# Merged DMA transposes for two head pairs in a pooled attention with a multiplicative feed-forward behind it

## The chip, the cores and the metric

The kernel runs on one core of a Trainium2 chip. The metric is the device time of one execution in microseconds (us), lower is better; the time before is the median of five executions.

## The reference

Attention with pooled queries, and then a feed-forward network without an activation function. Inputs are float32; the output is 4608 x 512 float32.

```python
B, H, S, D = 8, 8, 1152, 64
q_pool = q.reshape(B, H, S // 2, 2, D).mean(axis=3)            # 576 queries per head
scores = (1 / sqrt(D)) * q_pool @ k.transpose(0, 1, 3, 2)      # 576 x 1152 per head
attn = softmax(scores)
x = (attn @ v).transpose(0, 2, 1, 3).reshape(B * 576, 512)     # tokens x (head, D)
out = ((x @ w1) * (x @ w2)) @ w3 @ w_out                       # w1, w2: 512x1024, w3: 1024x1024, w_out: 1024x512
```

## The kernel before, in words

**Pairs.** Two heads at a time make a pair; there are 32 pairs (`NP`), four for each of the 8 batch entries. All matrix products are in fp16 with float32 accumulation. A pair's keys come in as 128 partitions x 2 heads x 9 rows x 64 (`kst`), its queries as 64 partitions x 2 x 18 x 64 (`qst`, two pairs share one tile of 128 partitions), its values like its keys (`vst`). GpSimd issues these loads (`load_k`, `load_q`, `load_v`); they convert float32 to fp16 on the way.

**Preparation of a pair.** VectorE copies the keys into `kc`, so that the two heads lie side by side, adds neighbouring queries into `qp` (`pool_q`), and copies the values into one of four standing tiles (`copy_v`). Keys and queries must then be transposed to `kT` and `qT`, with the head dimension on the partitions. For pairs 0 to 7 TensorE does it (`prep_first`, `prep_groups`). From pair 8 (`NPE`) on, `prep_dma` does it for two pairs at a time with DMA transposes, issued from SyncE's queue (SP): nine 128x128 tiles for the keys of the first pair (line 140), nine for the queries of both (line 143), nine for the keys of the second (line 140 again). `settled` (line 146) then lets GpSimd read one element of each of the three results, and only after that GpSimd issues the six loads of the two pairs that come next (`load_two`), so that these loads don't start beside the transposes.

**Scores and exponentials.** The main loop makes three chunks (`BURST`) of 512 columns each time: `scores` (line 248) multiplies keys by queries into a PSUM tile of tag `psc`, of which there are three, and ScalarE writes the exponentials into a ring `er` (line 258). A pair has 10.125 chunks.

**Attention times values.** `attend` (line 272) multiplies `er` by the values: 90 small matmuls a pair (2 heads x 9 key rows x 5 column groups), with a column of constants that gives the sum of the exponentials. The fifth column group overlaps the fourth: its upper 64 rows are the last 64 of the 576 queries. How many of these matmuls each turn of the loop issues stands in a list written out by hand (`PVS`). `normalize` (lines 285 and 289) divides by the sum and writes `xn`.

**Transposing the result.** `turn_x` issues two DMA transposes a pair: four 128x128 tiles (line 303) and a 64x128 piece for the last 64 queries (line 306). They write `xT`, the feed-forward network's input. For an odd pair this follows its `normalize`; even pairs from 8 on are put into `held` and turned at a later turn of the loop (line 552).

**Feed-forward.** Nine units of 512 tokens. A unit multiplies `xT` by w1 (`pa`) and w2 (`pb`, line 371); VectorE copies `pa` to `asb` (line 381) and multiplies it by `pb` into `gT` (line 383); then `gT` is multiplied by `T16`, the product of w3 and w_out that is made early (`pp`, line 389), VectorE scales it into `osb` (line 401), and SP stores it (line 410), two DMAs for every 128 tokens. The groups of up to seven units are put between the scores and the attention matmuls of the main loop, in one PSUM bank of their own ("F") or in one of the three `psc` slots ("X"); the last units run as a tail with ScalarE's help.

**What sets the order.** The program runs in manual order: every engine executes its instructions in the order in which the Python code emits them, and waits for the others by semaphores. So a wait of VectorE or of SP holds all that is behind it on that engine. Transposes and stores go through SP's queue, loads through GpSimd's; all of them share the core's 16 DMA engines.

Of the kernel before, what the change touches and what calls it, by code (L numbers as in the profile page):

```python
# [8 lines left out]
FP16 = mybir.dt.float16  # L9
# [5 lines left out]
SQ = 576  # L15
NJ = 9
# [3 lines left out]
VW = 66  # L20
# [3 lines left out]
def kernel(  # L24
# [11 lines left out]
    nc = tc.nc  # L36
    B, H, S, D = q.shape
# [5 lines left out]
    NP = B * H // 2  # L43
    SCL = 16.0
    NPE = 8
# [3 lines left out]
    const = ctx.enter_context(tc.tile_pool(name="const", bufs=1))  # L49
    stage = ctx.enter_context(tc.tile_pool(name="stage", bufs=4))  # L50
    ab = ctx.enter_context(tc.tile_pool(name="ab", bufs=4))
# [4 lines left out]
    xT = const.tile([128, NC, NT], FP16)  # L56
# [4 lines left out]
    er = const.tile([128, 2, RING], FP16)  # L61
    vts = [const.tile([128, 2, NJ, VW], FP16, name=f"vt{i}") for i in range(4)]

    ident = const.tile([128, 128], FP16)
    seen = const.tile([1, 3], FP16)

    ctx.enter_context(tc.manual_schedule())

# [1 line left out]
        nc.vector.memset(vt[:, :, :, D:VW], 1.0 / SCL)  # L70


    kst, vst, qst, kT, qT, qTs, qps = {}, {}, {}, {}, {}, {}, {}

    def load_q(P):
        b, h0 = P // 4, 2 * (P % 4)
# [36 lines left out]
    def pool_q(P, n=1):  # L113

        pp, o = P // 2, 64 * (P % 2)
        if P % 2 == 0:
            qps[pp] = ab.tile([128, NJ, 2, D], FP16, tag="qp", bufs=2, name="qp")
        r = slice(o, o + 64 * n)
        src = qst[pp][r].rearrange("p u (c two) d -> p u c two d", two=2)
        nc.vector.tensor_tensor(  # L120
            out=qps[pp][r].rearrange("p c u d -> p u c d"),
            in0=src[:, :, :, 0, :], in1=src[:, :, :, 1, :], op=ALU.add)

    def new_kq(P):
        kT[P] = ab.tile([128, NJ, 128], FP16, tag="kT", bufs=4, name="kT")
        if P % 2 == 0:
            qTs[P // 2] = ab.tile([128, NJ, 128], FP16, tag="qT", bufs=2, name="qT")
        o = 64 * (P % 2)
        qT[P] = qTs[P // 2][:, :, o:o + 64]

    def copy_v(P):
# [2 lines left out]
    def prep_dma(P):  # L134

        for p in (P, P + 1):
            new_kq(p)
            kc = ab.tile([128, NJ, 2, D], FP16, tag="kc", bufs=2, name="kc")
            nc.vector.tensor_copy(out=kc.rearrange("p j u d -> p u j d"), in_=kst.pop(p))
            nc.sync.dma_start_transpose(out=kT[p], in_=kc.rearrange("p j u d -> p (j u d)"))  # L140
            if p == P:
                pool_q(P, 2)
                nc.sync.dma_start_transpose(
                    out=qTs[P // 2], in_=qps[P // 2].rearrange("p c u d -> p (c u d)"))

    def settled(P):
        for n, t in enumerate((kT[P], qTs[P // 2], kT[P + 1])):
            nc.gpsimd.tensor_copy(out=seen[:, n:n + 1], in_=t[0:1, 0, 0:1])  # L148

    kcs = {}  # L150

    def new_kc(P):
        kcs[P] = ab.tile([128, NJ, 2, D], FP16, tag="kc", bufs=2, name="kc")
        return kcs[P]

    def prep_stage(P):
# [79 lines left out]
    def scores(c):  # L236
        t = psum.tile([128, 2, CH], FP32, tag="psc", bufs=3, name="psc")
        psc[c] = t
        g = c * CH
        while g < (c + 1) * CH:  # L240
            J = g // SQ
            P, j = divmod(J, NJ)
            f0 = g - J * SQ
            ln = min(SQ - f0, (c + 1) * CH - g)
            o = g - c * CH
            for u in range(2):
                s = slice(64 * u, 64 * u + 64)
                nc.tensor.matmul(t[:, u, o:o + ln].rearrange("p (c f) -> p c f", f=64), kT[P][s, j, :],  # L248
                                 qT[P][s, f0 // 64:(f0 + ln) // 64], start=True, stop=True)
            g += ln  # L250

    def expo(c):
        r = (c * CH) % RING
        g = (c - RING // CH + 1) * CH
        if g > 0:
            Pg, Jg = divmod((g - 1) // SQ, NJ)
            assert nb >= 90 * Pg + 45 + 5 * Jg + 5
        nc.scalar.activation(out=er[:, :, r:r + CH], in_=psc.pop(c), func=AF.Exp,  # L258
                             bias=0.0, scale=SCALE)

    po, xns = {}, {}

    def attend(n):

        P, m = divmod(n, 90)
        u, m = divmod(m, 45)
        j, i = divmod(m, 5)
        if m == 0:
            po[P, u] = psum.tile([128, 512], FP32, tag="po", bufs=1, name="po")
        f = 128 * i if i < 4 else SQ - 128  # L270
        r = ((P * NJ + j) * SQ) % RING + f
        nc.tensor.matmul(  # L272
            po[P, u][:, VW * i:VW * i + D + 1], er[:, u, r:r + 128],
            vts[P % 4][:, u, j, 0:D + 1],
            start=(m == 0), stop=(m == 44), skip_group_check=True)

# [5 lines left out]
    def normalize(P, u):  # L282
        acc = po.pop((P, u))[:, 0:5 * VW].rearrange("p (i w) -> p i w", w=VW)
        rz = ab.tile([128, 5, 1], FP32, tag="rz", bufs=2, name="rz")
        nc.vector.reciprocal(out=rz, in_=acc[:, :, D:D + 1])  # L285
        if u == 0:
            xns[P] = ab.tile([128, 5, 2, D], FP16, tag="xn", bufs=3, name="xn")
        xn = xns[P]
        nc.vector.tensor_tensor(  # L289
            out=xn[:, :, u, :], in0=acc[:, :, 0:D],  # L290
            in1=rz.to_broadcast([128, 5, D]), op=ALU.mult)
        if u == 0:
            return
        if P >= NPE and P % 2 == 0 and P < NP - 2:
            held.append(P)
        else:
            turn_x(P)

    def turn_x(P):
        xn = xns.pop(P)  # L300
        b, hp = divmod(P, 4)
        n0 = b * SQ
        nc.sync.dma_start_transpose(
            out=xT[:, hp, n0:n0 + 512].rearrange("p (i r) -> p i r", r=128),
            in_=xn[:, 0:4].rearrange("p i u d -> p (i u d)"))
        nc.sync.dma_start_transpose(
            out=xT[:, hp, n0 + 512:n0 + SQ].rearrange("p (i r) -> p i r", r=64),
            in_=xn[64:128, 4].rearrange("p u d -> p (u d)"))


    w3h = []
# [50 lines left out]
    def ffn_groups(t):  # L362
# [71 lines left out]
        out=ident, in_=ident, compare_op=ALU.not_equal, fill=1.0,  # L434
# [7 lines left out]
    load(3)  # L442
    load_w3(2)
    loaded, staged, prepped, copied = 4, 1, 1, 1
    held = []
    rest = prep_first()

    n_units = NT // 512
# [37 lines left out]
    def first_it(P):  # L486
        return P * PAIR // (CH * BURST)

    early = [(3, w3_group(0)), (4, w3_group(1))]
    for c in range(NF):  # L490
        t = (6, 7, 8, 9, 11, 12, 14, 15)[c]
# [14 lines left out]
    for it in range(NIT):  # L506
        at = it * BURST * CH / PAIR
        while early and it >= early[0][0]:
            queue.append(early.pop(0)[1])
        while next_unit < EARLY:  # L510
            last_b = (512 * (next_unit + 1) - 1) // SQ
            if it < 3 or reached[it - 2] < 360 * (last_b + 1):
                break
            gens.append(ffn_groups(next_unit))
            next_unit += 1
        for w in range(BURST):
            scores(BURST * it + w)
            expo(BURST * it + w)
        if it == 0:
            prep_rest(rest)  # L520
            load(4)
            load_w3(3)
            loaded = 5
        lead = 2 if staged < 4 else 3
        if staged < NPE and it >= first_it(staged) - lead:
            prep_stage(staged)
            staged += 1
            if staged <= 4:
                load(loaded)
                loaded += 1  # L530
            if staged <= 3:
                load_ffn(staged - 2)
        while 8 <= loaded < NPE + 2 and at >= loaded - 3.4:
            load(loaded)
            loaded += 1
        urgent = False
        if prepped < NPE:
            if it >= first_it(prepped) - (1 if prepped < 4 else 2):
                queue[0:0] = prep_groups(prepped)
                prepped += 1  # L540
                urgent = True
        elif prepped < NP and at >= prepped - 1.25:
            prep_dma(prepped)
            if loaded < NP:
                settled(prepped)
                load_two(loaded)
                loaded += 2
            prepped += 2
        if copied < NP and at >= copied - (1.2 if copied >= NPE else 0.6):
            copy_v(copied)  # L550
            copied += 1
        while held and at >= held[0] + 2.2:
            turn_x(held.pop(0))
        n = PVS[it]
        left = 45 - nb % 45
        brief = bool(queue) and queue[0][2] == 1
        a = left if left < n else 8 if brief and it > 8 and 8 < n < 40 and 8 < left else 0
        assert nb + n <= NPV and ready(nb + n - 1, BURST * it)
        pv(a)
        if head():  # L560
            group("F")
        if head() and (n < 40 or urgent or it < 17):
            group("X")
        pv(n - a)
        reached.append(nb)
    assert not held
    while nb < NPV:
        if head():
            group("F")
# [40 lines left out]
```

## Time and profile before

| | |
|---|---|
| time, median of 5 executions | 431.87 us (429.6 to 432.33) |
| profiled execution | 432.07 us, span 430.3 us |
| TensorE matmuls (PE) | 406.4 us, 94% of the span |
| ScalarE (ACT) | 326.6 us, 76% |
| VectorE (DVE) | 211.0 us, 49% |
| GpSimd (POOL) | 80.3 us, 19% |
| GpSimd's DMA queue (loads) | 48.3% of the 16 DMA engines' span |
| SP's DMA queue (transposes, stores) | 32.4% |
| granted TensorE clock, mean | 0.996 |

A time "busy" is the union of an engine's instructions. DMA issues count as no engine's work; SP's queue has a row for each, from the issue's start, and the trace tells when its data had landed. In rows of the timeline the bracket at the end says how long the engine had been idle and whose work ended that. Rows of a table by stretches give, after the length, busy us and instructions of PE, PE's weight loads, DVE, ACT and POOL, then the granted clock, the busy share of the DMA engines, and GB/s.

### The profile page before, as it was taken

The numbers are of one execution on the slowest core, as the hardware profiler recorded it, in microseconds if no ns is written. First come the engines' busy times: TensorE is split into PE (matmuls) and PEld (weight loads), VectorE is DVE, ScalarE is ACT, GpSimd is POOL, SyncE is SP. The second block draws the span as 40 slices with busy tenths as digits, with TensorE's granted clock in tenths as the row PEclk, the third lists the DMA queues.
The fourth block names the chain that finished last, engine by engine and source line by source line (L and its number), as shares of the span: only waits on it lengthen the run. The fifth ranks groups of instructions, "written<-read, shape, count | busy, mean of one in ns | idle before, by whom it ended". The sixth has DMA issues, their size and how long they took to land.

```text
span 430.3 us, 12736 instructions
## 1 busy us (share of the span) xinstructions
PE 406.4 (94%) x5432; PEld 269.5 (63%) x5432; DVE 211.0 (49%) x442; ACT 326.6 (76%) x355; POOL 80.3 (19%) x146
## 2 busy tenths in 40 slices
PE   3989999899999999799989999799999999999996
PEld 1667777666685577466765587466756776544443
DVE  1456565556536563456355554555465635623130
ACT  4898899879888888589878898788888899223332
POOL 8333321040401204030403012213004000000000
PEclk9999999999999999899999999999999999999999
DMA  8999999987895959997695969998958862040404
GB/s 126 205 208 200 188 180 172 152 153 123 126 201 114 179 88 165 218 148 126 98 201 104 161 122 185 169 189 119 218 116 122 112 147 40 15 100 12 99 1 98
DMA packets 95625, 59.16 MB, mean 137 GB/s; under 512 B 66256, under 2 KB 85968, under 8 KB 95568
## 3 DMA queue, kind: packets, MB, share of 16 engines
q0 software_dynamic: 26544, 33.56, 48.3%
q1 hardware_dynamic: 68864, 24.66, 32.4%
q8 instruction: 42, 0.69, 0.7%
q10 hardware_dynamic: 160, 0.13, 0.1%
q14 instruction: 15, 0.12, 0.1%
HBM read 67.11 MB, written 9.44 MB: 178 GB/s over the span
## 4 chain that ended last, share of the span: by engine, by line
PE 67%; DMA 26%; DVE 2%; POOL 2%; issue 2%; SPq 0%; ACT 0%; DVEq 0%; POOLq 0%
PE po L272 15%; PE pa L371 14%; PE pb L371 14%; PE psc L248 13%; PE pp L389 11%; DMA qst<-in_q_dram 7%; DMA vst<-in_v_dram 6%; DMA w2sb<-in_moe_w_dram 5%; DMA kst<-in_k_dram 4%; DMA out_dram<-osb 2%; DMA kT<-kc 2%; POOL kst L88 1%; DVE asb L381 1%; DVE osb L401 0%; POOL qst L80 0%
## 5 line engine op out<-in xcount | busy, mean ns | idle before, releaser
L258 ACT ACTIVATE er<-psc 128x1024 f16<-128x1024 f32 x324 | 308.0, 1025 | 53.5 <-PE psc L248 53.1
L272 PEld LDWEIGHTS <-er 128*128 128x128 f16 x2880 | 104.8, 98 | 23.6 <-issue 7.1
L272 PE MATMUL po<-vt,er 128*128 128x65 f16 x2880 | 111.9, 194 | 0.4 <-DVE xn L289 0.4
L248 PE MATMUL psc<-qT,kT 64*128 64x512 f16 (+7 forms) x1152 | 97.8, 291 | 13.1 <-DVE asb L381 4.0
L383 DVE TENSOR_TENSOR gT<-pb,asb 128x512 f16<-128x512 f32 x72 | 49.7, 691 | 52.9 <-PE pb L371 51.6
L371 PE MATMUL pa<-xT,w1sb 128*128 128x512 f16 x288 | 75.1, 383 | 0.0
L371 PE MATMUL pb<-xT,w2sb 128*128 128x512 f16 x288 | 74.1, 380 | 0.0
L248 PEld LDWEIGHTS <-kT 64*128 64x128 f16 x1152 | 46.3, 95 | 38.7 <-issue 19.1
L389 PE MATMUL pp<-T,gT 128*128 128x256 f16 (+1 forms) x488 | 67.9, 292 | 0.0
L389 PEld LDWEIGHTS <-gT 128*128 128x128 f16 x488 | 45.7, 98 | 18.5 <-issue 3.7
L381 DVE COPY asb<-pa 128x512 f32<-128x512 f32 x56 | 38.6, 689 | 34.6 <-PE pa L371 33.3
L371 PEld LDWEIGHTS <-w2sb 128*128 128x128 f16 x288 | 26.4, 98 | 32.7 <-issue 3.9
L371 PEld LDWEIGHTS <-w1sb 128*128 128x128 f16 x288 | 25.2, 98 | 30.6 <-issue 6.7
L401 DVE TENSOR_SCALAR osb<-pp 128x256 f32<-128x256 f32 x49 | 20.8, 424 | 39.9 <-PE pp L389 31.8
L148 POOL COPY seen<-kT 1x1 f16<-1x1 f16 x22 | 3.9, 177 | 185.5 <-DMA kT<-kc 185.5
L285 DVE RECIPROCAL rz<-po 128x5 f32<-128x5 f32 x64 | 12.4, 194 | 44.0 <-PE po L272 43.4
L289 DVE TENSOR_TENSOR xn<-po,rz 128x320 f16<-128x320 f32 x64 | 31.5, 492 | 2.2
L88 POOL DMA_DIRECT2D kst<-in_k_dram x33 | 24.1, 730 | 13.1 <-DMA kst<-in_k_dram 4.0
L95 POOL DMA_DIRECT2D vst<-in_v_dram x32 | 23.6, 750 | 13.1 <-DMA kst<-in_k_dram 3.8
L398 ACT ACTIVATE osb<-pp 128x512 f32<-128x512 f32 (+1 forms) x12 | 7.0, 580 | 24.2 <-PE pp L389 24.2
L379 ACT COPY asb<-pa 128x512 f32<-128x512 f32 x16 | 9.4, 586 | 16.4 <-PE pa L371 16.4
L80 POOL DMA_DIRECT2D qst<-in_q_dram x32 | 19.5, 616 | 10.0 <-DMA w2sb<-in_moe_w_dram 2.5
(39 smaller groups left out, 136.1 us busy)
## 6 DMA issues: line engine op xcount, KB each, us to landing
qst<-in_q_dram POOLq DMA_DIRECT2D x32, 288.0 KB, 7.0
vst<-in_v_dram POOLq DMA_DIRECT2D x32, 288.0 KB, 10.9
out_dram<-osb SPq DMA_DIRECT2D x70, 128.0 KB, 2.8
kst<-in_k_dram POOLq DMA_DIRECT2D x31, 288.0 KB, 7.6
w3h<-in_moe_w_dram POOLq DMA_DIRECT2D x4, 512.0 KB, 15.0
xT<-in_moe_w_out_dram POOLq DMA_DIRECT2D x2, 512.0 KB, 13.9
xT<-xn SPq DMA_TRANSPOSE x64, 4.8
w1sb<-in_moe_w_dram POOLq DMA_DIRECT2D x2, 512.0 KB, 16.8
```

The costliest lines, as they stand in the source:

```text
L80: nc.gpsimd.dma_start(out=qst[P // 2][o:o + 64].rearrange("p u t d -> p u (t d)"), in_=q[b, h0:h0 + 2].rearrange("u (p t) d -> p u (t d)", ...
L88: nc.gpsimd.dma_start(out=kst[P][:, :, js[0]:js[1], :], in_=k[b, h0:h0 + 2].rearrange("u (p j) d -> p u j d", j=NJ)[:, :, js[0]:js[1], :])
L95: nc.gpsimd.dma_start(out=vst[P].rearrange("p u j d -> p u (j d)"), in_=v[b, h0:h0 + 2].rearrange("u (p j) d -> p u (j d)", j=NJ))
L248: nc.tensor.matmul(t[:, u, o:o + ln].rearrange("p (c f) -> p c f", f=64), kT[P][s, j, :], qT[P][s, f0 // 64:(f0 + ln) // 64], start=True, ...
L258: nc.scalar.activation(out=er[:, :, r:r + CH], in_=psc.pop(c), func=AF.Exp, bias=0.0, scale=SCALE)
L272: nc.tensor.matmul(po[P, u][:, VW * i:VW * i + D + 1], er[:, u, r:r + 128], vts[P % 4][:, u, j, 0:D + 1], start=(m == 0), stop=(m == 44), ...
L289: nc.vector.tensor_tensor(out=xn[:, :, u, :], in0=acc[:, :, 0:D], in1=rz.to_broadcast([128, 5, D]), op=ALU.mult)
L371: nc.tensor.matmul(p, w[:, mc, ft * 128:ft * 128 + 128], xT[:, mc, t0:t0 + 512], start=(mc == 0), stop=(mc == NC - 1))
L381: nc.vector.tensor_copy(out=asb[ft], in_=p)
L383: nc.vector.tensor_mul(out=gT[:, ft, :], in0=p, in1=asb.pop(ft))
L389: nc.tensor.matmul(p[:, 0:n], gT[:, ft, 128 * i:128 * i + 128], T16[:, ft, n * s:n * s + n], start=(ft == 0), stop=(ft == NF - 1))
L401: nc.vector.tensor_scalar_mul(out=osb, in0=p[:, 0:n], scalar1=1.0 / (SCL * SCL))
```

## The change

Two neighbouring pairs share their tiles: `kc` and `kT` hold the keys of both (`kc` with one buffer in place of two of half the size, `kT` with two in place of four), `xn` holds both pairs' results (two buffers in place of three of half the size).

- `prep_dma` copies the keys of both pairs first, issues one transpose of 18 tiles for them, and then pools the queries and issues the one of nine tiles for these.
- `settled` reads one element of the keys and one of the queries.
- The attention matmuls of an odd pair put their column groups one place further in PSUM, so that the fifth group comes first; in `xn` the last 64 tokens of the even pair and of the odd one then lie beside each other.
- `held` and `turn_x` are gone. After the odd pair's `normalize` three transposes are issued: four tiles of the even pair, four of the odd one, and one 64x256 piece for the last 64 tokens of both.

TensorE's and ScalarE's instructions keep their order and number. VectorE's keep their number, with the second copy of keys ahead of the pooling of queries.

```diff
     def new_kq(P):
-        kT[P] = ab.tile([128, NJ, 128], FP16, tag="kT", bufs=4, name="kT")
         if P % 2 == 0:
+            kTs[P // 2] = ab.tile([128, 2, NJ, 128], FP16, tag="kT", bufs=2, name="kT")
             qTs[P // 2] = ab.tile([128, NJ, 128], FP16, tag="qT", bufs=2, name="qT")
         o = 64 * (P % 2)
+        kT[P] = kTs[P // 2][:, P % 2]
         qT[P] = qTs[P // 2][:, :, o:o + 64]
...
         for p in (P, P + 1):
             new_kq(p)
-            kc = ab.tile([128, NJ, 2, D], FP16, tag="kc", bufs=2, name="kc")
-            nc.vector.tensor_copy(out=kc.rearrange("p j u d -> p u j d"), in_=kst.pop(p))
-            nc.sync.dma_start_transpose(out=kT[p], in_=kc.rearrange("p j u d -> p (j u d)"))
-            if p == P:
-                pool_q(P, 2)
-                nc.sync.dma_start_transpose(
-                    out=qTs[P // 2], in_=qps[P // 2].rearrange("p c u d -> p (c u d)"))
+            nc.vector.tensor_copy(out=new_kc(p).rearrange("p j u d -> p u j d"), in_=kst.pop(p))
+        nc.sync.dma_start_transpose(
+            out=kTs[P // 2].rearrange("p t j f -> p (t j) f"),
+            in_=kc2[P // 2].rearrange("p t j u d -> p (t j u d)"))
+        pool_q(P, 2)
+        nc.sync.dma_start_transpose(
+            out=qTs[P // 2], in_=qps[P // 2].rearrange("p c u d -> p (c u d)"))
 
     def settled(P):
-        for n, t in enumerate((kT[P], qTs[P // 2], kT[P + 1])):
+        for n, t in enumerate((kT[P], qT[P])):
             nc.gpsimd.tensor_copy(out=seen[:, n:n + 1], in_=t[0:1, 0, 0:1])
...
     def new_kc(P):
-        kcs[P] = ab.tile([128, NJ, 2, D], FP16, tag="kc", bufs=2, name="kc")
+        if P % 2 == 0:
+            kc2[P // 2] = ab.tile([128, 2, NJ, 2, D], FP16, tag="kc", bufs=1, name="kc")
+        kcs[P] = kc2[P // 2][:, P % 2]
         return kcs[P]
...
         f = 128 * i if i < 4 else SQ - 128
+        x = (i + P % 2) % 5
         r = ((P * NJ + j) * SQ) % RING + f
         nc.tensor.matmul(
-            po[P, u][:, VW * i:VW * i + D + 1], er[:, u, r:r + 128],
+            po[P, u][:, VW * x:VW * x + D + 1], er[:, u, r:r + 128],
...
-        if u == 0:
-            xns[P] = ab.tile([128, 5, 2, D], FP16, tag="xn", bufs=3, name="xn")
-        xn = xns[P]
+        if u == 0 and P % 2 == 0:
+            xns[P // 2] = ab.tile([128, 2, 5, 2, D], FP16, tag="xn", bufs=2, name="xn")
+        xn = xns[P // 2]
         nc.vector.tensor_tensor(
-            out=xn[:, :, u, :], in0=acc[:, :, 0:D],
+            out=xn[:, P % 2, :, u, :], in0=acc[:, :, 0:D],
             in1=rz.to_broadcast([128, 5, D]), op=ALU.mult)
-        if u == 0:
+        if u == 0 or P % 2 == 0:
             return
-        if P >= NPE and P % 2 == 0 and P < NP - 2:
-            held.append(P)
-        else:
-            turn_x(P)
-
-    def turn_x(P):
-        xn = xns.pop(P)
-        b, hp = divmod(P, 4)
+        b, hp = divmod(P - 1, 4)
         n0 = b * SQ
+        for h in range(2):
+            nc.sync.dma_start_transpose(
+                out=xT[:, hp + h, n0:n0 + 512].rearrange("p (i r) -> p i r", r=128),
+                in_=xn[:, h, h:h + 4].rearrange("p i u d -> p (i u d)"))
         nc.sync.dma_start_transpose(
-            out=xT[:, hp, n0:n0 + 512].rearrange("p (i r) -> p i r", r=128),
-            in_=xn[:, 0:4].rearrange("p i u d -> p (i u d)"))
-        nc.sync.dma_start_transpose(
-            out=xT[:, hp, n0 + 512:n0 + SQ].rearrange("p (i r) -> p i r", r=64),
-            in_=xn[64:128, 4].rearrange("p u d -> p (u d)"))
+            out=xT[:, hp:hp + 2, n0 + 512:n0 + SQ],
+            in_=xn.rearrange("p h i u d -> p (h i) (u d)")[64:128, 4:6].rearrange("p a f -> p (a f)"))
...
-        while held and at >= held[0] + 2.2:
-            turn_x(held.pop(0))
```

More of the change, by code (lines that the diff above doesn't have):

```diff
@@ L64 @@
     ident = const.tile([128, 128], FP16)
-    seen = const.tile([1, 3], FP16)
+    seen = const.tile([1, 2], FP16)
     ctx.enter_context(tc.manual_schedule())
@@ L70 @@
         nc.vector.memset(vt[:, :, :, D:VW], 1.0 / SCL)
-    kst, vst, qst, kT, qT, qTs, qps = {}, {}, {}, {}, {}, {}, {}
+    kst, vst, qst, kT, qT, kTs, qTs, qps = {}, {}, {}, {}, {}, {}, {}, {}
     def load_q(P):
@@ L137, in prep_dma @@
             new_kq(p)
-            kc = ab.tile([128, NJ, 2, D], FP16, tag="kc", bufs=2, name="kc")
-            nc.vector.tensor_copy(out=kc.rearrange("p j u d -> p u j d"), in_=kst.pop(p))
-            nc.sync.dma_start_transpose(out=kT[p], in_=kc.rearrange("p j u d -> p (j u d)"))
-            if p == P:
-                pool_q(P, 2)
-                nc.sync.dma_start_transpose(
-                    out=qTs[P // 2], in_=qps[P // 2].rearrange("p c u d -> p (c u d)"))
+            nc.vector.tensor_copy(out=new_kc(p).rearrange("p j u d -> p u j d"), in_=kst.pop(p))
[5 more added lines that the diff above has]
+            out=qTs[P // 2], in_=qps[P // 2].rearrange("p c u d -> p (c u d)"))
     def settled(P):
-        for n, t in enumerate((kT[P], qTs[P // 2], kT[P + 1])):
+        for n, t in enumerate((kT[P], qT[P])):
             nc.gpsimd.tensor_copy(out=seen[:, n:n + 1], in_=t[0:1, 0, 0:1])
-    kcs = {}
+    kcs, kc2 = {}, {}
     def new_kc(P):
-        kcs[P] = ab.tile([128, NJ, 2, D], FP16, tag="kc", bufs=2, name="kc")
+        if P % 2 == 0:
+            kc2[P // 2] = ab.tile([128, 2, NJ, 2, D], FP16, tag="kc", bufs=1, name="kc")
+        kcs[P] = kc2[P // 2][:, P % 2]
         return kcs[P]
@@ L444 @@
     loaded, staged, prepped, copied = 4, 1, 1, 1
-    held = []
     rest = prep_first()
@@ L565 @@
         reached.append(nb)
-    assert not held
     while nb < NPV:
```

## The prediction

> **What bounds the kernel now.** I read the page first: busy times, then the slices.
>
> ```profile
> span 430.3 us, 12736 instructions
> PE 406.4 (94%) x5432; PEld 269.5 (63%) x5432; DVE 211.0 (49%) x442; ACT 326.6 (76%) x355; POOL 80.3 (19%) x146
> q1 hardware_dynamic: 68864, 24.66, 32.4%
> ```
>
> TensorE is the limit: 24 us of the span are without it, of which some 7.7 lie ahead of its first scores and 2.4 behind its end. So I asked TensorE's waits for the rest:
>
> ```profile
> PE psc L248 <- DVE asb L381: 4.0, 2, 2.2
> ...
> PE psc L248 <- DVE gT L383: 3.0, 1, 3.0
> PE psc L248 <- DVE osb L401: 1.1, 1, 1.1
> ```
>
> After the start the only waits above 0.6 us are four: at 84.2 (1.76 us), 174.6 (3.00), 218.2 (1.10), 269.2 (2.25). TensorE and ScalarE execute the same order before and after in the built program, so the time moves only through these four, or through a new one. The timelines say what stands behind them:
>
> ```profile
> 80.33 0.45 DVE L139 COPY kc<-kst 128x1152 f16<-128x1152 f16 x1
> 83.51 0.76 DVE L120 TENSOR_TENSOR qp<-qst 128x1152 f16<-128x1152 f16 x1 [2.73 <-DMA qst<-in_q_dram]
> 84.18 0.45 DVE L139 COPY kc<-kst 128x1152 f16<-128x1152 f16 x1
> 85.99 0.40 PE L248 MATMUL psc<-qT,kT 64*128 64x128 f16 x4 [1.76 <-DVE asb L381]
> ...
> 165.88 1.75 SPq L303 DMA_TRANSPOSE xT<-xn  x1
> 172.07 1.39 SPq L140 DMA_TRANSPOSE kT<-kc  x1
> 173.83 0.46 DVE L139 COPY kc<-kst 128x1152 f16<-128x1152 f16 x1 [1.06 <-DMA kst<-in_k_dram]
> 175.66 0.46 DVE L132 COPY vt<-vst 128x1152 f16<-128x1152 f16 x1 [1.37 <-DMA vst<-in_v_dram]
> 177.57 0.61 PE L248 MATMUL psc<-qT,kT 64*128 64x128 f16 x4 [3.00 <-DVE gT L383]
> ```
>
> VectorE is in order: a copy that waits for a load holds up asb and gT behind it, and these hold the PSUM slot that the next scores need. At 84, 174 and 269 it is thus a late load; at 218 an output buffer whose store landed late. The stretches of two microseconds give one more price:
>
> ```profile
> 176.00:178.00 2.00, 0.43 (x4) 0.13 (x3) 1.86 (x5) 0.34 (x1) 0.00 (x0) 0.88 1.66 307
> 178.00:180.00 2.00, 2.00 (x10) 0.80 (x9) 0.14 (x1) 1.02 (x1) 0.00 (x0) 0.50 0.82 151
> 180.00:182.00 2.00, 2.00 (x49) 1.92 (x48) 0.81 (x2) 0.00 (x0) 0.35 (x2) 0.76 1.17 239
> ```
>
> After the 3.00 us wait the granted clock is 0.50 for 3.41 us (177.54 to 180.95), which costs half of that, 1.7 us. After the waits of 1.76 and 2.25 us it stays at 1.00.
>
> **Part by part.** The sum is made against the profiled execution: 432.07 us, its span of 430.3 and 1.8 around it; the median of five is 431.87.
>
> *Fewer transposes.* 100 become 72: 12 fewer of keys (24 to 12), 16 fewer of xT (64 to 48). Each takes SP's queue 1.2 to 1.3 us, so some 35 us of SP, but SP bounds nothing by itself; and the moved packets stay the same 59904 of 256 bytes. Zero by itself. What counts is where packets stand beside the loads.
>
> *Head, at 84.* Pair 4's xT was issued at 68.4, into the loads of pairs 8 and 9; its 576 packets (36 on each of 16 engines) alternate there with load packets and take 31 ns each (18 ns alone), so 1.1 us of the loads' time. In the built program SP issues it behind the transposes of pairs 8 and 9. Those loads are back to back, so kst of pair 9 (landed 82.49) and qst (83.42) come 1.1 us sooner. VectorE's order also becomes kc, kc, qp: the second kc (0.37 us from start to start of the next) falls into the wait for qst. So asb comes 1.1 + 0.4 = 1.5 us sooner and 0.3 of 1.76 remain. Ends: -0.4 (the order alone) to -1.76. Taken: -1.5. TensorE is without a gap for 90 us after it, so this carries through.
>
> *The merged chain: keys of two, then queries.* Where no load is near, the three old transposes landed 3.4, 4.9 and 6.2 us after the first issue, paced by SP (prep of 12, 20, 26, 28). The same 27 tiles are 216 packets per engine, 3.9 us at 18 ns; with 1.0 until the first packet and 0.5 after the last this gives 5.4. So the queries, now last, land between 5.4 and 6.2, and GpSimd, which lets the next six loads go after that, starts them up to 0.8 sooner. In the preps of 14, 22 and 30 a 16 KB instruction packet (1.1 to 1.3 us on one engine) falls into the transposes; before, the third landed at 7.04, 6.56 and 7.02. After: 5.4 + 1.0 to 1.3 = 6.4 to 6.7. But pair P needs keys and queries: before the last it needs landed at 5.74, 5.21 and 5.71, its first score stood at 6.04, 6.05 and 6.06. So pairs 14, 22 and 30 would wait 0.4 to 0.6 us. At 14 and 22 this costs nothing: the waits at 174 and 269, set by loads that follow the same transposes, absorb it. At 30 no load follows: +0.5, ends 0 and +1.0.
>
> *At 174.* V of pair 16 (landed 175.64) sets the end. The loads start 0.35 to 0.65 sooner (7.04 to 6.4-6.7). Pair 12's xT, issued at 165.88 into them, is moved behind the next transposes: -1.1. But four stores of 64x512, which SP issued only behind it at 169.2 to 171.3 and which landed after V (177.3 to 179.3), now come first: 4 packets of 2 KB on each engine per store, 96 ns each, 0.8 for two, 1.5 for four. A store waited some 4 us from issue to its first packet in such a stretch, so I count two: -1.1 + 0.8 = -0.3; with four -1.1 + 1.5 = +0.4. Sum -0.65 to -0.95 with two, about 0 with four; the second kc and qp (1.1 us) fit into the 1.8 us between that K and V landing. Taken: -0.5, ends -1.2 and +0.5.
>
> *Clock.* The wait would be 2.5 us. 3.00 brought the drop, 2.25 did not; it lies midway, so half of 1.7: -0.85, ends 0 and -1.7. The one run of before at 429.6 is about what the kernel would take without the drop. The Trainium skill, page "TensorE: Matmul & The Clock Gate", section "Part 1", has the array fall to half clock after at least one idle window of about 3.4 us. By that, 3.00 us would not have brought it, and the trace shows that it did; by the page alone the term would be 0 and the sum -2.1.
>
> *At 218.* The prep of 18 had its third transpose land at 7.8 us, behind an instruction packet that came at 5.8. A chain that ends at 5.4 is ahead of it, the loads start up to 2.3 us sooner and have gone further when the stores of 210.4 are issued, whose landing at 218.74 made the wait. Ends 0 and -1.1; taken half: -0.5.
>
> *At 269.* As at 174, but the loads gain only 6.56 to 6.4, and three to four stores are ahead of V: -0.7 to +0.5, taken -0.1.
>
> *Nothing for the rest.* Pair's xT issued together: the even one is issued as soon as SP comes to it; all units start 6 us or more after their last xT, and in the tail pair 31's lands near 381.1 with its first reader at 384.8. One buffer of two for kc: its readers end 6 us or more ahead. PV's turned columns: same matmuls. GpSimd's dropped copy: 0.18 us.
>
> Sum: -1.5 + 0.5 - 0.5 - 0.85 - 0.5 - 0.1 = -2.95, so 432.07 - 2.95 = 429.1.
>
> **Rivals.** *Slower: the merged transpose itself is late.* No row shows 18 tiles in one. If its two halves don't overlap as two transposes do, it lands at twice 3.3 and the queries 1.4 later: 8.0. Pairs 12, 20, 28 and 30 have their first scores at 6.97, 6.48, 6.34 and 6.06: waits of 1.0, 1.5, 1.7 and 1.9; the loads behind 14 and 22 come 1.0 and 1.4 later. Together 8.5, less 1.5 of the head: +7.0, 439.1. It decides from a landing of the queries at about 6.8 us in quiet preps, where its waits eat the head's 1.5. For it: use stands only 0.3 to 0.8 us behind the landing in the tightest preps. Against it: packets of successive transposes follow without a gap.
>
> *No change: stores fill the hole.* All four stores are ahead of V at 174 and 269 and loads start no sooner (+0.4 each), the head gains the order's 0.4 alone, pair 30 waits 0.5: +0.9, 433.0, clock drop kept. For it: stores wait on SP directly behind xT.
>
> *It does not do what it says:* even and odd xT are together in SP's list but not in time, since the even one's wait is over earlier and SP passes it. In the built program pairs 4, 12 and 20 move behind a prep, 8, 16, 24 and 28 behind stores, and the others stay. I count it so already; it is in the forecast.
>
> **How the numbers follow.** The forecast has 0.57, stores 0.23, the late transpose 0.20. A difference of 0.5% (2.2 us) is about what a measurement of this kernel tells from none. The forecast's best ends add up to 1.76 + 1.2 + 1.7 + 1.1 + 0.7 = 6.5 (425.6), its worst to +1.6. It is faster by over 0.5% in 0.45, same in 0.12 of its 0.57; the stores' case same in 0.16, slower in 0.05, faster in 0.02; the late transpose slower in 0.19, same in 0.01. So faster 0.47, same 0.29, slower 0.24. The range 426 to 434.5 leaves out the best end and most of the late transpose. The forecast's own range is 425.6 to 433.6.
>
> **What would show it.** Right: kst and qst of pair 9 land about 1 us sooner ahead of the wait at 84, which shrinks below 0.7; queries land 5.4 to 6.2 us after the merged keys' issue; no clock of 0.50 near 178. Wrong: score waits on the keys' or queries' DMA at pairs 12, 20, 28; V of pair 16 later than 12.6 us after the first load of its six; waits at 174 and 269 above 3 us, the second then with a clock drop of its own.

## The result: slower by 0.75%, and the profile after

The changed kernel takes 434.14 us (median of 27 executions, 430.82 to 437.23); the kernel before, run beside it, takes 431.86 us (46 executions). The ratio is 1.0075, 95% interval 1.0056 to 1.0094: slower by some 3.2 us, where 2.95 us less had been forecast. The ratio is of fast executions alone, those within 1.5% of the kernel's fastest (37 of 46 before, all 27 after); the medians of all differ by 2.3 us. The profiled execution of after took 436.63 us.

The page after, the same three lines as before:

```profile
span 434.9 us, 12640 instructions
PE 408.6 (94%) x5432; PEld 270.6 (62%) x5432; DVE 211.4 (49%) x442; ACT 326.6 (75%) x355; POOL 78.3 (18%) x135
...
q1 hardware_dynamic: 67968, 24.66, 30.9%
```

The work is the same: 5432 matmuls, the same 24.66 MB through SP's queue in 896 packets less (packets of 4 bytes; those of 256 bytes are 59904 in both). TensorE is busy for 2.2 us longer, mostly by one more stretch at half clock (1.7 us). The rest must be in waits. TensorE's waits after (us in total, times, longest):

```profile
PE psc L251 <- DMA qT<-qp: 3.7, 5, 2.2
...
PE psc L251 <- DVE asb L379: 2.4, 1, 2.4
PE psc L251 <- DVE gT L381: 2.3, 1, 2.3
PE psc L251 <- DVE osb L399: 1.3, 1, 1.3
```

The first line is new: scores wait for the transposed queries, 2.21 us at pair 12, then 0.55, 0.16, 0.54 and 0.27 at pairs 14, 20, 22 and 30. The wait at 84 is gone (`asb` has one wait where it had two), and those at 175, 218 and 270 are still there. The same TensorE instruction stands, against before, 2.27 us earlier at 84, but 0.10 later at 138.7, 1.43 later at 256, 3.2 later behind the wait at 270 with its half clock, 3.66 later at the end. The head's gain was there and was gone at pair 12.

The timeline after around pair 12 (VectorE, SP's queue, TensorE):

```profile
115.63 11.54 SPq L408 DMA_DIRECT2D out_dram<-osb  x8
...
126.41 0.82 DVE L139 COPY kc<-kst 128x1152 f16<-128x1152 f16 x2
127.22 2.59 SPq L301 DMA_TRANSPOSE xT<-xn  x2
129.86 1.23 SPq L304 DMA_TRANSPOSE xT<-xn  x1
131.27 2.69 SPq L140 DMA_TRANSPOSE kT<-kc  x1
134.07 1.38 SPq L144 DMA_TRANSPOSE qT<-qp  x1
138.76 0.50 PE L251 MATMUL psc<-qT,kT 64*128 64x256 f16 x6 [2.21 <-DMA qT<-qp]
```

Both copies of keys are done at 127.23, but SP comes to the keys' transpose at 131.27, behind eight stores and three transposes of `xT`, and to that of the queries at 134.07. The queries landed at 138.72, which is 7.45 us after the keys' issue. TensorE wanted them at 136.55, 5.28 after it.

### The profile page after: what moved, and what is told of

The parts are those of the page before. It is cut to its first block, busy times and chain, and to the rows that moved or that the text cites. A ratio compares the mean times of both kernels' runs of the same rounds, so it can differ in the third digit from the quotient of the medians.

```text
span 434.9 us, 12640 instructions
## 1 busy us (share of the span) xinstructions
PE 408.6 (94%) x5432; PEld 270.6 (62%) x5432; DVE 211.4 (49%) x442; ACT 326.6 (75%) x355; POOL 78.3 (18%) x135
## 3 DMA queue, kind: packets, MB, share of 16 engines
q1 hardware_dynamic: 67968, 24.66, 30.9%
## 4 chain that ended last, share of the span: by engine, by line
PE 70%; DMA 12%; ACT 5%; SPq 5%; DVE 3%; issue 3%; POOL 1%; DVEq 0%; POOLq 0%; ACTq 0%
PE po L276 15%; PE psc L251 14%; PE pa L369 13%; PE pb L369 13%; PE pp L387 9%; ACT er L261 5%; DMA vst<-in_v_dram 5%; DMA qT<-qp 4%; SPq L140 3%; PE pT L353 3%; DMA out_dram<-osb 2%; SPq L304 1%; DMA qst<-in_q_dram 1%; PE w3t L341 1%; DVE kc L139 1%
## 5 line engine op out<-in xcount | busy, mean ns | idle before, releaser
L369 PE MATMUL pb<-xT,w2sb 128*128 128x512 f16 x288 | 75.0, 383 | 0.0
L149 POOL COPY seen<-kT 1x1 f16<-1x1 f16 x11 | 1.9, 176 | 198.0 <-DMA kT<-kc 198.0
```

The source lines that it names most:

```text
L369: nc.tensor.matmul(p, w[:, mc, ft * 128:ft * 128 + 128], xT[:, mc, t0:t0 + 512], start=(mc == 0), stop=(mc == NC - 1))
```

## The experiments

Ratios are to the kernel before on the same chip. "Use" below is the first score's start after the first issue of its prep, less the wait, so it says when TensorE would have used the keys and queries.

**Both kernels once more.** One profile of each doesn't tell which waits belong to the kernel. Edit: none.

> The kernel before, unchanged, profiled a second time, for how far one profile speaks for the kernel. If the waits belong to the kernel: again near 84 (1.8 us), 175 (3.0), 218 (1.1), 270 (2.3), each within 0.5 us. If to the run: the head's wait is below 1 us and the others move by more than 0.5 us.

> The changed kernel, unchanged, profiled a second time. Theory A: waits on queries again at pairs 12, 14 and 22 or 30, 3 us or more in total, that of pair 12 the longest at about 2 us; no wait near 84. If they belong to the run, the total is below 2 us or pair 12 has none.

Before took 430.11 us (span 428.3), after 438.21 us (span 436.4). The scores' wait on queries in this second profile of after:

```profile
PE psc L251 <- DMA qT<-qp: 4.3, 5, 2.3
```

The wait of 2.29 us at pair 12 and the four small ones came again in after (0.49, 1.03, 0.33 and 0.18). In before the wait at 84 did not: the queries of pair 9 were loaded by 81.18, where it had been 83.42, with pair 4's `xT` in its old place both times. So the size of that wait differs from execution to execution. The two waits for values (near 174 and 269) are in all four profiles: 3.00 and 2.25, 2.56 and 2.73 before; 2.34 and 2.44, 3.02 and 2.32 after. This profile of before also has TensorE where after has it (`xn` of pair 9 at 126.05 against 126.00), so SP's queue can be compared row by row:

```profile
119.73 1.33 SPq L303 DMA_TRANSPOSE xT<-xn  x1
...
126.45 0.45 DVE L139 COPY kc<-kst 128x1152 f16<-128x1152 f16 x1
126.56 1.94 SPq L303 DMA_TRANSPOSE xT<-xn  x1
128.55 1.23 SPq L306 DMA_TRANSPOSE xT<-xn  x1
129.94 1.30 SPq L140 DMA_TRANSPOSE kT<-kc  x1
131.41 1.30 SPq L143 DMA_TRANSPOSE qT<-qp  x1
```

Keys are issued at 129.94 and queries at 131.41, in after at 131.27 and 134.07: 1.33 and 2.66 us later for the same TensorE. The first difference is pair 8's `xT`. Before, it went out at 119.73, between the two groups of stores; now it stands behind both, with pair 9's. The second difference is the queries' place behind 18 tiles of keys.

**Each part alone.** The change with keys and queries transposed as before (9 tiles, queries, 9 tiles), so that only the joint `xT` is left:

```diff
-            nc.vector.tensor_copy(out=new_kc(p)..., in_=kst.pop(p))
-        nc.sync.dma_start_transpose(out=kTs[P // 2]..., in_=kc2[P // 2]...)
-        pool_q(P, 2)
-        nc.sync.dma_start_transpose(out=qTs[P // 2], in_=qps[P // 2]...)
+            kc = new_kc(p)
+            nc.vector.tensor_copy(out=kc..., in_=kst.pop(p))
+            nc.sync.dma_start_transpose(out=kT[p], in_=kc...)
+            if p == P:
+                pool_q(P, 2)
+                nc.sync.dma_start_transpose(out=qTs[P // 2], in_=qps[P // 2]...)
```

> The changed kernel with its keys and queries transposed as before (nine tiles of keys, the queries, nine tiles of keys, three reads in the settling step); the joint xT transposes stay. Theory A, the merged keys: the 18-tile issue holds SP for 2.7 us and the queries land behind 27 tiles, 6.1 to 7.5 us after the first issue instead of 4.8 to 5.7; that makes TensorE's five waits on the queries (3.7 us in the changed kernel's profile). Then these waits fall to 0.6 us or less in total and the time to 430 to 431.6 us. Theory B, the moved xT: the even pairs' transposes, now behind stores, push the keys back on SP. Then 2 us or more of these waits stay and the time stays within 1 us of the changed kernel's 434.1.

And before with the merged keys alone (`kc` and `kT` for two pairs and both copies of keys first, as in the change), `xT` and `held` as they were:

```diff
-            nc.sync.dma_start_transpose(out=kT[p], in_=kc...)
-            if p == P:
-                pool_q(P, 2)
-                nc.sync.dma_start_transpose(out=qTs[P // 2], in_=qps[P // 2]...)
+        nc.sync.dma_start_transpose(out=kTs[P // 2]..., in_=kc2[P // 2]...)
+        pool_q(P, 2)
+        nc.sync.dma_start_transpose(out=qTs[P // 2], in_=qps[P // 2]...)
```

> The kernel before with the merged keys alone; xT transposes per pair and held as before. Theory A: waits on queries at pairs 14, 22 and 30 of about 0.5 us each, at pair 12 up to 0.5 (its first score stands 6.97 us after the first issue there), no gain at the head but VectorE's order (0.4): 432 to 433.5 us. Theory B: nothing is pushed back, so no waits on queries above 0.3 us, and the time is that of before, 431.9, or up to 1 us less.

The joint `xT` alone: 432.71 us, ratio 1.0036 (1.0001 to 1.0071). The merged keys alone: 431.91 us, 1.0030 (1.0000 to 1.0060). Waits on queries, in this order:

```profile
PE psc L251 <- DMA qT<-qp: 1.1, 1, 1.1
```

```profile
PE psc L251 <- DMA qT<-qp: 1.0, 2, 0.7
```

With the joint `xT` alone the only wait on queries is at pair 12: keys issued at 132.05, use 5.2 us after it, queries landed 6.27 after it. With the merged keys alone pair 12 doesn't wait: queries landed 6.05 after the keys' issue, use 6.75. Its waits are at 22 (0.74) and 30 (0.28). Neither half makes the 2.2 us. In the second profile of before pair 12 has 1.7 us of slack: queries landed 4.80 after the keys' issue, use 6.48. The joint `xT` issues the keys 1.33 later, and then a 16 KB packet of the DMA queue that the profile names "instruction" falls into the transposes: it comes 5.7 us after the keys' issue in both profiles of before, 4.1 to 4.4 after it in the four profiles with the joint `xT` and this prep in its old place (after twice, the joint `xT` alone, and the run under "One DMA, or the order?"), and in these four the queries of pair 12 land 1.2 to 1.6 us later than in the same kernel's quiet preps. Together that makes the 1.1 us of this run. The queries' place behind 18 tiles adds 1.2, which by itself the slack still covers.

Of the expectations for the joint `xT` alone neither came in full: the waits fell to 1.1 us, between the 0.6 of one side and the 2 of the other, and the time lies between theirs too. For the merged keys alone the time would fit either theory; waits above 0.3 us speak for theory A, though they came at 22 and 30 and not at 14.

**Undoing the pair's `xT` only.** The change with the even pair's four tiles put into `held` and turned at the old turn of the loop; keys merged, last 64 tokens joint:

```diff
+        if P % 2 == 0:
+            if P >= NPE and P < NP - 2:
+                held.append(P)
+            else:
+                turn_x(P)
+            return
+        turn_x(P)
...
-        for h in range(2):
-            nc.sync.dma_start_transpose(out=xT[:, hp + h, ...], in_=xn[:, h, h:h + 4]...)
...
+        while held and at >= held[0] + 2.2:
+            turn_x(held.pop(0))
```

> The changed kernel with the four-tile xT transposes of even pairs back where they were (pair 8's between the two groups of stores, held by the main loop); keys stay merged, the last 64 tokens of two pairs stay in one transpose. Both parts are needed for the wait at pair 12 (27 tiles ahead of the queries' landing, and pair 8's xT on SP ahead of the keys, 1.3 us): then its first score stands again 6.5 us or more after the first issue without a wait, the wait there is 0.8 us or less, waits on queries in total 1 to 2 us, time 431 to 432.8. If pair 8's xT has no share: the wait at 12 stays at 2 us or more and the time above 433.5.

431.18 us, ratio 1.0008 (0.9975 to 1.0041), apart from the change's own interval. The timeline at pair 12, SP and TensorE:

```profile
127.46 1.59 SPq L314 DMA_TRANSPOSE xT<-xn  x1
129.10 1.23 SPq L307 DMA_TRANSPOSE xT<-xn  x1
130.50 2.66 SPq L140 DMA_TRANSPOSE kT<-kc  x1
133.28 1.29 SPq L144 DMA_TRANSPOSE qT<-qp  x1
136.99 0.83 PE L251 MATMUL psc<-qT,kT 64*128 64x192 f16 x12
```

The row of six matmuls with a bracket of 2.21 has merged into one of twelve without a bracket: no wait. Queries landed 6.04 us after the keys' issue, use 6.82. Waits of 0.66, 0.45 and 0.20 at pairs 14, 22 and 30 stay, which belong to the merged keys.

**Covering pair 12 only.** The change, with the prep of pair 12 one turn of the loop sooner:

```diff
-        elif prepped < NP and at >= prepped - 1.25:
+        elif prepped < NP and at >= prepped - (1.55 if prepped == 12 else 1.25):
```

> The changed kernel with the preparation of pair 12 alone one turn sooner. The wait at pair 12 (2.2 us, sometimes with a clock drop of 1.7) is gone, the small ones at 14, 22 and 30 (some 0.5 us each) and those on V near 175 and 271 stay: 2.2 to 3.5 us less than the changed kernel, 430.6 to 432. If the waits on V take over what this one gives back, less than 1 us is gained and these waits are above 3.5 us.

431.65 us, ratio 1.0019 (0.9989 to 1.0049), also apart from the change's. Use moved to 12.85 us, the wait at pair 12 is gone, and the others are 0.59, 1.00, 0.34 and 0.26 at 14, 20, 22 and 30. The sooner prep moves by more than a turn: SP now comes to the keys at 123.23, ahead of the last two stores and of all three transposes of `xT`, 8 us sooner than in the change. So undoing one wait, with the clock behind it, takes back most of the loss; the two waits for values were 2.09 and 2.00 here, so a part may be theirs.

**One DMA, or the order?** The change with the keys as two transposes of nine tiles, both still ahead of the queries:

```diff
-        nc.sync.dma_start_transpose(
-            out=kTs[P // 2].rearrange("p t j f -> p (t j) f"),
-            in_=kc2[P // 2].rearrange("p t j u d -> p (t j u d)"))
...
+            kc = new_kc(p)
...
+            nc.sync.dma_start_transpose(out=kT[p], in_=kc.rearrange("p j u d -> p (j u d)"))
```

> The changed kernel with the keys as two transposes of nine tiles, but both ahead of the queries: the merge is undone, its order kept. If the order is what costs (pair P needs its queries, and these come behind 18 tiles of keys either way), the queries land 6.0 to 6.3 us after the first issue in quiet preps and the time is within 0.7 us of the changed kernel's 434.1, waits on queries 3 us or more. If the one 18-tile DMA costs by itself, the queries land 5.4 or less after the first issue, the waits fall to 1.5 us or less and the time to 432 or less.

436.2 us, ratio 1.0133 (1.0083 to 1.0183). Waits on queries add up to 4.8 us; the rows at pair 12:

```profile
131.68 2.72 SPq L141 DMA_TRANSPOSE kT<-kc  x2
134.51 1.31 SPq L143 DMA_TRANSPOSE qT<-qp  x1
139.20 0.68 PE L250 MATMUL psc<-qT,kT 64*128 64x256 f16 x6 [2.23 <-DMA qT<-qp]
```

Two DMAs of nine tiles hold SP for 2.72 us, the one of 18 for 2.69, and where nothing disturbs them the queries land at 6.07 to 6.22 us against 6.02 to 6.25. So it is the order, the queries behind 18 tiles of keys, and not the size of the DMA. The landings and waits came as the order's side expected; the time did not, 2.1 us above the change's 434.1 where 0.7 had been allowed. This version is no faster than the change; whether it is slower is not settled, since the intervals overlap.

**All preps in danger sooner.** In the change and in the kernel before, the preps of 12, 14, 20, 22, 28 and 30 one turn sooner:

```diff
-        elif prepped < NP and at >= prepped - 1.25:
+        elif prepped < NP and at >= prepped - (1.55 if prepped % 8 in (4, 6) else 1.25):
```

> The changed kernel with the preparations of pairs 12, 14, 20, 22, 28 and 30 one turn of the main loop (about 3.3 us) sooner. Theory A: the late landing is then covered, TensorE's waits on queries vanish (below 0.2 us in total), the loads that follow go 3 us sooner and the waits on V near 175 and 271 shrink by 1.5 us or more, with fewer clock drops: 426 to 430 us. Rival: the sooner copies of keys of 14 and 22 now wait for their own loads (keys of pair 15 landed at 152.2, the copy would stand at 149.5) and hold VectorE: new waits of 1 to 2 us near 150 and 245, the time 432 or more.

> The kernel before, nothing merged, with the preparations of pairs 12, 14, 20, 22, 28 and 30 one turn of the main loop sooner. Theory A: the merge costs only where its late landing is not covered; with the same cover the kernel without it gains from the sooner loads alone and ends where the changed kernel with sooner preparations ended, 425.3 us, within 1.5 us. Rival: the merge costs or gains by itself (fewer issues on SP, fewer transposes beside loads); then the two sooner kernels differ by more than 1.5 us, with the unmerged one at 427 or more if merging helps, at 423.5 or less if it hurts.

After with it: 425.3 us, ratio 0.9862 (0.9821 to 0.9903). Before with it: 424.89 us, 0.9825 (0.9783 to 0.9867). In both, the use of these pairs moves to 11.6 us or more behind the first issue, and the waits on queries and those near 174 and 269 are gone. What is left above 0.8 us is one wait of 1.0 us for `osb` in after, and 2.08 for `osb` and 1.14 at 83.5 in before. The medians differ by 0.4 us, the ratios by 0.4% (each against before on its own chip), with intervals that overlap. So where the landing is covered, no cost and no gain of the merge can be seen, to some 2 us: 28 DMAs fewer are worth no time that these runs could tell. After with it was faster than theory A's 426 to 430; the rival's waits near 150 and 245 did not come. The Trainium skill, page "DMA: Bandwidth & Descriptors", section "Rules for kernel authors", advises to coalesce many small transfers into one large one, and names 64 KB as small. Of what is merged here only the 64x128 pieces of `xT` are below that (16 KB; nine tiles of keys are 288 KB). These runs show no gain of merging in this place.

**The best of it.** Since the wait that is left there is for an output buffer, the change with sooner preps and four buffers `osb` for three:

```diff
-                    osbs[i] = ffp.tile([128, dm], FP32, tag="osb", bufs=3, name="osb")
+                    osbs[i] = ffp.tile([128, dm], FP32, tag="osb", bufs=4, name="osb")
```

> The changed kernel with the sooner preparations and a fourth buffer for the output rows, for a version without the wait of 1.0 us near 218 that the sooner kernel still has: 1 us less than its 425.3, or up to 2.7 where that wait brings a clock drop: 422.5 to 424.5. If stores aren't what VectorE waits for there, within 0.5 us of 425.3.

421.74 us (six executions, 421.43 to 421.97), ratio 0.9786 (0.9737 to 0.9834), the fastest of all, and 0.8 us below the range that was expected. That last part no run here explains. Its page:

```profile
span 419.5 us, 12631 instructions
PE 403.6 (96%) x5432; PEld 268.1 (64%) x5432; DVE 211.8 (50%) x442; ACT 326.2 (78%) x355; POOL 78.1 (19%) x135
```

Behind 20 us TensorE has no wait above 0.7 us. The spread went with the waits: 0.5 us here over six executions, 3.5 and 4.3 over six each with the sooner preps alone, 6.4 in after over 27, 8.9 in before over 46.

**The head alone.** Before, with pair 4's `xT` issued behind the prep of pairs 8 and 9, as the change does:

```diff
-        if P >= NPE and P % 2 == 0 and P < NP - 2:
+        if P == 4:
+            held.append(P)
+        elif P >= NPE and P % 2 == 0 and P < NP - 2:
             held.append(P)
...
-        while held and at >= held[0] + 2.2:
+        while held and at >= held[0] + (2.75 if held[0] == 4 else 2.2):
```

> The kernel before with one move: pair 4's xT transposes stand behind the preparation of pairs 8 and 9. The prediction's head term: the loads of pair 9 land 1.1 us sooner relative to TensorE, the wait near 84 shrinks from 1.76 to some 0.6, time 430.2 to 431 (0.9 to 1.3 us below before). Rival: the wait at the head in the one profile was that run's own (loads of other kernels that keep this xT in place landed 1.6 us sooner too); then the time is that of before within 0.5 us.

430.47 us, ratio 0.9965 (0.9934 to 0.9997): 1.5 us less, by the interval 0.1 to 2.9. No wait at 84; the waits for values are 2.7 and 2.6, and the granted clock stays at 1.00 behind both. All 13 profiles agree on the wait at 84: with pair 4's `xT` in its old place it was 1.76 and none in before, 1.14 in before with sooner preps, 0.56 with the merged keys alone, 0.75 with the even pair held; in the eight with it behind the prep there is none.

## Why the prediction was wrong

**The step that failed is "Nothing for the rest".** It has pair 8's `xT` issued "as soon as SP comes to it" and checks when its readers need it, which was right: no reader was late. What it did not price is what stands behind it on SP. The move past the second group of stores puts it directly ahead of the keys of pair 12 and pushes these by 1.33 us. The prediction had listed the move ("8, 16, 24 and 28 behind stores") under a rival and counted it for the loads only. Putting the even pairs' four tiles back leaves 0.08% of the 0.75% (the interval reaches to 0.41%). In the wait at pair 12 it is the larger part: 1.33 us for the later issue and 1.2 to 1.6 for the instruction packet that the later issue meets, against 1.2 for the order.

**The merged chain was sized too low.** Undisturbed, 5.4 to 6.2 us were given, and 6.02 to 6.25 came, at the upper end. It was not the packets that paced the chain, but SP: 18 tiles are issued in 2.69 us, as long as two times nine, so the queries are issued 2.8 us behind the keys, and land 3.2 to 3.3 after that, much as nine tiles alone do (3.3 to 3.4 before). In the first profile pair 20, landing at 6.02, is 0.1 us short, and pair 28 at 6.25 is in time. At pair 12 the landing was 7.45 and 7.62, with the 16 KB instruction packet that now falls into it. The forecast counted +0.5 at pair 30, and the term measured 3.7 and 4.3 us over five pairs. Its second half failed too: the waits at 14 and 22 were to be absorbed by those at 174 and 269, and these didn't shrink (sums of the two: 5.25 and 5.29 us before, 4.78 and 5.34 after).

**Head, -1.5:** the mechanism exists, and the head alone measured 1.5 us less. But the wait of 1.76 us, from which the term was taken, was absent in the second profile of before and 0.56 to 1.14 in the three others that keep this `xT` in place, so -1.5 was read from a wait that few executions have in full. That the run of the head alone came out at 1.5 is in part luck: its interval reaches from 0.1 to 2.9. In the profile after, VectorE's order is as forecast, with both copies and the pooling without a gap:

```profile
80.00 0.82 DVE L139 COPY kc<-kst 128x1152 f16<-128x1152 f16 x2
80.73 0.75 DVE L120 TENSOR_TENSOR qp<-qst 128x1152 f16<-128x1152 f16 x1
```

**At 174, 218 and 269:** -0.5, -0.5 and -0.1 were forecast. The sum of the two outer ones is within 0.6 us in all four profiles, and the wait at 218 was 1.10 or none before, 1.29 and 0.82 after. No gain shows in any of the three. With the keys merged and the even pairs' `xT` in their old place the two outer waits add up to 3.74 (merged keys alone) and 3.44 us (even pair held), 1.5 to 1.9 less than before: the merged keys may have brought some of the forecast gain, and the joint `xT` taken it back. One profile of each does not show it.

**Clock, -0.85: the rule was wrong.** It went by the length of a wait: 3.00 us brings half clock, 2.25 does not. The runs contradict it: 2.08 brought it in one, 2.74 did not in another. What fits every one of the 13 profiles is a grid. The stretches between changes of the granted clock are whole multiples of 3.413 us (before: 46, 1 and 73 of them; after: 46, 1, 27, 1, 46). At full clock, idle time of TensorE of 1.96 us or more within one window of this grid was always followed by half clock in the next, and 1.90 or less never (the ends of matmuls are modelled, so the last hundredths are not sure). One window at half clock with 1.59 us idle was followed by another. Three windows of after (length, then PE busy; the granted clock stands behind POOL's):

```profile
136.86:140.27 3.41, 1.51 (x20) 1.02 (x21) 0.53 (x2) 1.84 (x3) 1.27 (x4) 1.00 0.23 51
...
174.40:177.82 3.42, 1.08 (x24) 0.62 (x20) 2.16 (x6) 2.48 (x3) 0.00 (x0) 1.00 1.22 188
177.82:181.23 3.41, 3.41 (x32) 1.93 (x32) 1.17 (x2) 1.02 (x1) 0.18 (x1) 0.50 1.16 243
```

The first window has 1.90 us idle, and the clock stays: the wait at pair 12 began 0.3 us ahead of a boundary. In the second profile of after 2.05 us of the same wait lie in one window, and the next is at 0.50:

```profile
134.80:138.21 3.41, 1.36 (x34) 1.09 (x33) 1.06 (x2) 1.64 (x2) 0.18 (x1) 1.00 0.92 95
138.21:141.62 3.41, 3.17 (x21) 1.59 (x21) 0.69 (x2) 1.94 (x2) 2.75 (x5) 0.50 0.30 37
```

And where the head alone was changed, a wait of 2.74 us is cut by a boundary into 1.12 and 1.62 and costs no clock:

```profile
170.43:173.84 3.41, 2.29 (x30) 1.21 (x29) 0.91 (x3) 3.13 (x5) 0.00 (x0) 1.00 1.22 200
173.84:177.25 3.41, 1.79 (x28) 1.11 (x28) 2.44 (x6) 1.67 (x2) 0.00 (x0) 1.00 1.19 226
```

The Trainium skill, page "TensorE: Matmul & The Clock Gate", "Part 1", says that the window is 3413 ns and runs freely, and the trace agrees in both (46 x 3.413 = 157.0 us, and the grid begins at 18.3 to 20.9 us, differently in each run). It also says that an idle window is needed; here one that is 57% idle is enough. By the grid a wait of L us, placed at random, is followed by half clock with a chance of (1.46 + L - 1.95) / 3.41: 0.50 for 2.2, 0.59 for 2.5, 0.74 for 3.0. This is an estimate, and by it the step from 3.0 to 2.5 was worth 0.15 x 1.7 = 0.26 us and not 0.85, while a new wait of 2.2 us costs 0.85 on top.

**The sum again,** with measured sizes: pair 12's wait +2.2 and its clock +0.85, the other four waits +1.5 to +2.0, values -0.2 (5.27 to 5.06 in the mean), head -1.76 to 0. This gives 2.6 to 4.9 us, and the ratio says 3.2. That waits and clock carry it, to some 2 us, can be tried on every run: the profiled time less TensorE's waits before scores (those above 0.15 us, behind 60 us) and less half of what it works at half clock is 421.0 to 423.2 us in all 13 profiles, whose times range from 421.4 to 438.2.

**What was right:** that TensorE's waits, with the clock behind them, carry what the time can gain or lose; that 28 fewer DMAs are worth nothing that can be seen by themselves; that pairs 14, 22 and 30 would wait 0.4 to 0.6 us (0.55, 0.54 and 0.27, then 0.49, 0.33 and 0.18); and that use stands close behind the landing in the tightest preps. That last was the slower rival's ground, but its mechanism did not occur: the merged transpose is as quick as two, and the queries at 6.8 us or more, from which it was to decide, occurred, where use is that close, only at pair 12 in the first profile. That 434.14 us lies inside the range of 426 to 434.5 is luck: the width was there for other causes, and no term of the sum led to it.

What stays open: how the 0.75% divides. The joint `xT` alone cost 0.36% with a wait on queries of 1.1 us, the merged keys alone 0.30% with 1.0, and the change with the even pair held 0.08% with 1.3; intervals of 0.3% to either side cannot tell these apart, and the waits for values (3.0 and 3.5 in the first) vary from run to run by as much.

## What to carry to other kernels

Before DMAs of one queue are merged or regrouped, list for each transfer two times, counted from its issue: when it lands and when it is used. A merge makes the landing later for whatever is put behind it; a step that is moved in front of other issues makes these go out later, so that their use comes sooner after the issue. Small losses on each side meet in one wait. A transfer that is moved is priced by who stands behind it on its queue, not only by its own reader. If a wait is to be judged from one profile, take a second one first; and where use stands within 1 or 2 us of landing, issuing one turn sooner (here worth 1.4 to 1.8%) is the better edit.

## What the runs showed of the hardware

- The clock's decision by a grid of 3.413 us, with a threshold between 1.90 and 1.96 us of idle time in one window. It turns equal waits into different times (2.21 us at pair 12 without half clock, 2.29 with it), and by that accounts for part of the spread of a kernel's executions.
- A DMA transpose from SBUF to SBUF, where nothing delays it, holds SP's queue for 1.2 us with 4 tiles, 1.3 with 9, 2.7 with 18, so merging two of 9 saves SP nothing.
- An instruction packet of 16 KB (0.9 to 2.7 us on one DMA engine, nine in ten of them under 1.5) comes at nearly the same place of TensorE's progress (near pair 12 between matmul 1867 and 1898 in the nine profiles without a sooner prep). At pair 12 a transpose that was under way landed 1.2 to 1.6 us later. A prep that slides against TensorE can slide into it.
